# mLSTM cell and mixture of depths on one core: decay exponents built by matmul instead of by broadcast loads

## The chip, the cores and the metric

The kernel runs on one core of a Trainium2 chip. The metric is the time of one execution on the device, in microseconds (us). Before the change it is 265.21 us, the median of three runs (263.96 to 266.42). Engines are named as in the profile: PE (TensorE, with PEld for its weight loads), DVE (VectorE), ACT (ScalarE), POOL (GpSimd), SP (SyncE, which here only issues transfers).

## The reference

Two stages follow one another. The first is an mLSTM cell over B=4 batches, H=8 heads, S=768 time steps and head size D=40, with a running maximum `m` that keeps the exponents in bounds:

```python
for t in range(S):
    m_new = np.maximum(f_gate[:, :, t] + m, i_gate[:, :, t])
    f_stab = np.exp(f_gate[:, :, t] + m - m_new)
    i_stab = np.exp(i_gate[:, :, t] - m_new)
    m = m_new
    C = f_stab * C + i_stab * outer(vt, kt)
    n = f_stab * n + i_stab * kt
    y[t] = sigmoid(o_gate[t]) * (C @ qt) / max(|n . qt|, 1)
```

The heads are laid side by side: x has 4 x 768 rows of 320. The second stage gives each row a score x . w_gate, picks the 128 highest rows of each batch, and replaces each picked row by x + sigmoid(score) * (relu(x @ w1) @ w2), with w1 320x1024 and w2 1024x320. All is float32.

## The kernel before

**Tiling.** The time axis is cut into NT=6 chunks of L=128 steps, so there are 24 steps (b, c) in the outer loop (L371), batch after batch. Within a chunk the recurrence is written as matmuls: a masked weight W (source step by target step, per head) multiplies k.q, and the product P times v gives the chunk's own share; the state C, carried from chunk to chunk, gives the rest. A column of ones beside v (D1 = 41) carries the normaliser n.

**Prologue (L84 to L159).** The gates of all 32 (batch, head) rows lie on 32 partitions. For each of the six chunks DVE scans F (sums of f), a = i - F and Mg (running maximum of a), ACT takes the exponentials r and wk, PE transposes a, wk and r to columns (`cols`), and Mg with r's last value behind it is stored to a scratch `M_d[c]` in DRAM.

**Loads (L95 to L103, L350).** For a step, SP issues k, q and v (160 KB each, in runs of 160 bytes) and then `Mb`, which reads eight rows of `M_d` into all 128 partitions (516 KB). NB=4 buffers, AHEAD=2 steps ahead. The o gates of a batch are six further loads (`so`), issued at the batch's start for the first batch and at c = 3 for the next; ACT turns them into sigmoids (L364).

**A step, `mlstm_chunk` (L174 to L255).** POOL masks Mb (L177). ACT makes W in eight exponentials, one per head (L181). PE transposes k and q (L188), ACT copies them out (L189). PE computes pS (L198), DVE multiplies with W into P (L200). PE reads the state, pI (L207), and DVE scales it by r into `num` (L210). POOL scales v (wv, L215), PE makes the state's addition pC (L221), DVE decays C by the value carried in Mb and adds pC (L229, L231). PE makes pH from P and v (L236) and DVE adds it to `num` (L240). DVE forms the denominator and its reciprocal (L243 to L246), POOL multiplies it with the o gate (`sor`, L248), DVE writes x (L249) and its score (L252). POOL issues two stores of x, one to a scratch `x_d` and one to the output (L255).

**Ranking and the picked rows.** `compare` (L257) adds a chunk's scores to comparisons (`ge`, L265), one step late. `ranks` (L269) and `gather` (L289) pick the rows and fetch them from `x_d` (L301); `layer1` (L307) and `layer2` (L338) are the two products, and L345 scatters the rows to the output. For batches 0 and 1 this is done inside the next batch's steps. After the last step come batch 2's layer1, then batch 3's ranks, batch 2's layer2, batch 3's gather and its two layers (L402 to L406).

**Order.** The engines take their instructions in order. A scheduler in the framework orders the instructions of each engine at build time from the order of the program; buffers of a pool rotate, and an instruction that writes a buffer waits for the last reader of its previous content. PSUM tiles of one tag share two buffers: `t` holds pt, `a` holds pI, pC and pH, `m` the rest, and pS has two of its own.

Of the kernel before, what the change touches and what calls it, by code (L numbers as in the profile page):

```python
# [27 lines left out]
def kernel(  # L28
# [35 lines left out]
    NB = 4  # L64
    GE = [L * u * (u + 1) // 2 for u in range(NT + 1)]
    HALVES = [slice(0, 64), slice(64, 128)]
    AHEAD = 2

    assert S == NT * L and D < DP and H == 2 * NP and BH <= 128 and F_ == NFC * 128 and 0 < capacity < S <= 2048
# [14 lines left out]
    f_sb = gate.tile([BH, NT, L], FP, name="f_sb")  # L84
    i_sb = gate.tile([BH, NT, L], FP, name="i_sb")
    nc.sync.dma_start(out=f_sb, in_=f_gate.rearrange("b h (c p) -> (b h) c p", p=L))
    nc.sync.dma_start(out=i_sb, in_=i_gate.rearrange("b h (c p) -> (b h) c p", p=L))
# [3 lines left out]
    for n in range(NB):  # L91
        nc.gpsimd.memset(qk_t[n][:, :, :, D:DP], 0.0)
        nc.gpsimd.memset(v_t[n][:, :, D:DP], 1.0)

    def load_chunk(b, c):  # L95
        n = (b * NT + c) % NB
        t = slice(c * L, (c + 1) * L)
        for j, src in enumerate((k, q)):
            nc.sync.dma_start(out=qk_t[n][:, j, :, 0:D], in_=src[b, :, t, :].rearrange("h p d -> p h d"))  # L99
        nc.sync.dma_start(out=v_t[n][:, :, 0:D], in_=v[b, :, t, :].rearrange("h p d -> p h d"))  # L100
        Mb = work.tile([128, H, L + 1], FP, name="Mb", bufs=NB)
        nc.sync.dma_start(out=Mb, in_=_bcast(M_d[c][b * H:(b + 1) * H, :], 128))
        return qk_t[n], v_t[n], Mb  # L103

    ident = const.tile([128, 128], FP, name="ident")
    make_identity(nc, ident)
    iota_i = const.tile([128, capacity], I32, name="iota_i")
    nc.gpsimd.iota(iota_i, pattern=[[1, capacity]], channel_multiplier=0)
    iota_f = const.tile([128, capacity], FP, name="iota_f")
    nc.vector.tensor_copy(out=iota_f, in_=iota_i)  # L110

    token_i = const.tile([128, NT], I32, name="token_i")
    nc.gpsimd.iota(token_i, pattern=[[L, NT]], channel_multiplier=1)
    token = const.tile([128, NT], HF, name="token")
    nc.vector.tensor_copy(out=token, in_=token_i)
    later = const.tile([128, NT], FP, name="later")
    nc.vector.tensor_scalar(out=later, in0=token_i, scalar1=-1.0, scalar2=float(S - 1), op0=OP.mult, op1=OP.add)
    earlier = const.tile([128, NT * L], BF, name="earlier")
    nc.gpsimd.memset(earlier, 1.0)
    nc.gpsimd.affine_select(out=earlier[:, S - L:], in_=earlier[:, S - L:], compare_op=OP.is_gt, fill=0.0, base=0,  # L120
                            pattern=[[-1, L]], channel_multiplier=1)
    ones_b = const.tile([128, 1], BF, name="ones_b")
    nc.gpsimd.memset(ones_b, 1.0)
    xe_t = [const.tile([128, NDC * 128], FP, name=f"xe{n}") for n in range(2 * len(SLOTS))]
    n_xe = [0]
    for n in range(len(xe_t)):
        nc.gpsimd.memset(xe_t[n], 0.0)
    x_d = [dram.tile([S, DM], FP, name=f"x_d{b}") for b in range(B)]
    ones = const.tile([BH, L], FP, name="ones")
    nc.vector.memset(ones, 1.0)  # L130


    F = gate.tile([BH, NT, L], FP, name="F")
    a = gate.tile([BH, NT, L], FP, name="a")
    Mg = gate.tile([BH, NT, L + 1], FP, name="Mg")
    r = gate.tile([BH, NT, L], FP, name="r")
    wk = gate.tile([BH, NT, L], FP, name="wk")
    m = gate.tile([BH, NT + 1], FP, name="m")
    nM = gate.tile([BH, NT], FP, name="nM")
    nc.vector.memset(m[:, 0:1], -BIG)  # L140
    M_d, cols = [], []
    for c in range(NT):
        nc.vector.tensor_tensor_scan(out=F[:, c, :], data0=ones, data1=f_sb[:, c, :], initial=0.0,
                                     op0=OP.mult, op1=OP.add)
        nc.vector.tensor_tensor(out=a[:, c, :], in0=i_sb[:, c, :], in1=F[:, c, :], op=OP.subtract)
        nc.vector.tensor_tensor_scan(out=Mg[:, c, 0:L], data0=ones, data1=a[:, c, :], initial=m[:, c:c + 1],
                                     op0=OP.mult, op1=OP.max)
        nc.vector.tensor_tensor(out=m[:, c + 1:c + 2], in0=F[:, c, L - 1:L], in1=Mg[:, c, L - 1:L], op=OP.add)
        nc.vector.tensor_scalar(out=nM[:, c:c + 1], in0=Mg[:, c, L - 1:L], scalar1=-1.0, scalar2=None, op0=OP.mult)
        nc.scalar.activation(out=r[:, c, :], in_=Mg[:, c, 0:L], func=AF.Exp, bias=m[:, c:c + 1], scale=-1.0)  # L150
        nc.scalar.activation(out=wk[:, c, :], in_=a[:, c, :], func=AF.Exp, bias=nM[:, c:c + 1], scale=1.0)
        nc.vector.tensor_copy(out=Mg[:, c, L:L + 1], in_=r[:, c, L - 1:L])
        M_d.append(dram.tile([BH, L + 1], FP, name=f"M_d{c}"))
        nc.scalar.dma_start(out=M_d[c], in_=Mg[:, c, :])
        pc = ps_t.tile([128, 3, BH], FP, name="pc", tag="t")
        for j, row in enumerate((a, wk, r)):
            nc.tensor.transpose(pc[:, j, :], row[:, c, :], ident[0:BH, 0:BH])
        cols.append(const.tile([128, 3, BH], FP, name=f"cols{c}"))
        nc.vector.tensor_copy(out=cols[c], in_=pc)  # L159
# [5 lines left out]
    nc.gpsimd.dma_start(out=wg, in_=_bcast(moe_w_gate, 128))  # L165
# [8 lines left out]
    def mlstm_chunk(b, c, qk, v1, Mb, C, so, x, sc):  # L174
        hs = slice(b * H, (b + 1) * H)
        k_n, q_n = qk[:, 0], qk[:, 1]
        nc.gpsimd.affine_select(out=Mb[:, :, 0:L], in_=Mb[:, :, 0:L], compare_op=OP.is_ge, fill=BIG, base=0,  # L177
                                pattern=[[0, H], [1, L]], channel_multiplier=-1)
        W = work.tile([128, NP, 2, L], FP, name="W")
        for h in range(H):  # L180
            nc.scalar.activation(out=W[:, h // 2, h % 2, :], in_=Mb[:, h, 0:L], func=AF.Exp,  # L181
                                 bias=cols[c][:, 0, b * H + h:b * H + h + 1], scale=-1.0)

        qkT = work.tile([128, 2, NP, L], FP, name="qkT", bufs=2)
        for j in range(2):
            pt = ps_t.tile([128, NP, L], FP, name="pt", tag="t")
            for p in range(NP):
                nc.tensor.transpose(pt[:, p, :], qk[:, j, 2 * p:2 * p + 2, :].rearrange("s a d -> s (a d)"), ident)  # L188
            nc.scalar.copy(out=qkT[:, j], in_=pt)  # L189


# [3 lines left out]
        for p in range(NP):  # L195
            for j in range(2):
                e = HALVES[j]
                nc.tensor.matmul(pS[j][:, p, :], qkT[e, 0, p, :], qkT[e, 1, p, :], start=True, stop=True)  # L198
        for j in range(2):
            nc.vector.tensor_tensor(out=P[:, :, j, :], in0=pS[j], in1=W[:, :, j, :], op=OP.mult)  # L200

        num = None
        if c > 0:
            pI = ps_a.tile([128, H, DP], FP, name="pI", tag="a")
            for p in range(NP):
                for t in HALVES:
                    nc.tensor.matmul(pI[t, 2 * p:2 * p + 2, :].rearrange("t a d -> t (a d)"), qkT[:, 1, p, t],  # L207
                                     C[:, p].rearrange("e a d -> e (a d)"), start=True, stop=True)
            num = work.tile([128, H, D1], FP, name="num")
            nc.vector.tensor_tensor(out=num, in0=pI[:, :, 0:D1], op=OP.mult,  # L210
                                    in1=cols[c][:, 2, hs].unsqueeze(2).to_broadcast([128, H, D1]))

        if c < NT - 1:
            wv = work.tile([128, H, D1], FP, name="wv", bufs=2)
            nc.gpsimd.tensor_tensor(out=wv, in0=v1[:, :, 0:D1], op=OP.mult,  # L215
                                    in1=cols[c][:, 1, hs].unsqueeze(2).to_broadcast([128, H, D1]))
# [5 lines left out]
            decay = Mb.rearrange("p (n a) t -> p n a t", a=2)  # L222
            for j in range(2):
                e = slice(j * DP, j * DP + D)
                Cj, pj = C[e, :, j, 0:D1], pC[e]
                if c == 0:
                    nc.vector.tensor_copy(out=Cj, in_=pj)
                else:
                    nc.vector.tensor_tensor(out=Cj, in0=Cj, op=OP.mult,  # L229
                                            in1=decay[e, :, j, L:L + 1].to_broadcast([D, NP, D1]))  # L230
                    nc.vector.tensor_tensor(out=Cj, in0=Cj, in1=pj, op=OP.add)  # L231

        pH = ps_a.tile([128, H, DP], FP, name="pH", tag="a")
        for h in range(H):
            for t in HALVES:
                nc.tensor.matmul(pH[t, h, :], P[:, h // 2, h % 2, t], v1[:, h, :], start=True, stop=True)  # L236
        if num is None:
            num = pH
        else:
            nc.vector.tensor_tensor(out=num, in0=num, in1=pH[:, :, 0:D1], op=OP.add)  # L240
# [192 lines left out]
```

## Time and profile before

| | |
|---|---|
| median of three runs | 265.21 us |
| profiled execution | 263.01 us |
| its span, first to last instruction | 261.3 us |
| busy: PE, DVE, ACT, POOL | 189.9, 148.7, 120.1, 105.5 us |
| mean granted TensorE clock | 0.88 of full |
| moved by DMA | 41.07 MB, 107085 packets, of which 101328 under 512 bytes |

The profiled execution took 1.7 us more than its span and 2.2 us less than the median. The first x is written at 25.5 us, the second at 48.2, the last (of 24) at 217.7; what follows to 261.3 us is the tail. In lists of groups a row gives line, engine, operation, output and inputs with shapes, count, busy us with mean ns of one, and the engine's idle time before such instructions. In timelines the two leading numbers are start and duration in us.

### The profile page before, as it was taken

The numbers are of one execution on the slowest core, as the hardware profiler recorded it, in microseconds if no ns is written. First come the engines' busy times: TensorE is split into PE (matmuls) and PEld (weight loads), VectorE is DVE, ScalarE is ACT, GpSimd is POOL, SyncE is SP. The second block draws the span as 40 slices with busy tenths as digits, with TensorE's granted clock in tenths as the row PEclk, the third lists the DMA queues.
The fourth block names the chain that finished last, engine by engine and source line by source line (L and its number), as shares of the span: only waits on it lengthen the run. The fifth ranks groups of instructions, "written<-read, shape, count | busy, mean of one in ns | idle before, by whom it ended". The sixth has DMA issues, their size and how long they took to land.

```text
span 261.3 us, 6263 instructions
## 1 busy us (share of the span) xinstructions
PE 189.9 (73%) x2402; PEld 160.6 (61%) x2402; DVE 148.7 (57%) x443; ACT 120.1 (46%) x304; POOL 105.5 (40%) x155
## 2 busy tenths in 40 slices
PE   0498204875987968899799687998969862982980
PEld 0376103764966856887687576976859752961950
DVE  5813303687767998831779799347876985021000
ACT  2484049776568455760556578237633300000000
POOL 8435322635365455643643655443354222003001
PEclk9999855797799988799999979999995995798696
DMA  8979899999799899996599999717533121001000
GB/s 119 147 272 222 288 205 226 224 194 238 163 238 264 198 203 230 238 185 227 102 177 215 221 211 258 222 75 152 130 81 113 41 75 50 3 0 50 3 0 25
DMA packets 107085, 41.07 MB, mean 157 GB/s; under 512 B 101328, under 2 KB 101520, under 8 KB 107056
## 3 DMA queue, kind: packets, MB, share of 16 engines
q1 hardware_dynamic: 103392, 28.61, 55.8%
q0 software_dynamic: 3376, 11.96, 13.6%
q8 instruction: 19, 0.31, 0.5%
q10 hardware_dynamic: 288, 0.10, 0.2%
q14 instruction: 10, 0.08, 0.1%
HBM read 32.05 MB, written 8.62 MB: 156 GB/s over the span
## 4 chain that ended last, share of the span: by engine, by line
issue 23%; DMA 20%; DVE 19%; PE 12%; SPq 10%; POOL 10%; ACT 2%; POOLq 1%; ACTq 0%; DVEq 0%
DMA Mb<-M_d 10%; POOL sor L248 5%; SPq L350 5%; PE pH L236 3%; DVE P L200 3%; DVE x L249 3%; SPq L100 3%; DMA out_dram<-x 3%; PE ph L331 2%; DMA qk<-in_k_dram 2%; SPq L99 2%; DVE ge L265 2%; POOL Mb L177 2%; DMA so<-in_o_gate_dram 2%; DVE C L229 2%
## 5 line engine op out<-in xcount | busy, mean ns | idle before, releaser
L181 ACT ACTIVATE W<-Mb,cols 128x128 f32<-128x128 f32 x192 | 61.2, 392 | 22.8 <-POOL Mb L177 11.8
L236 PE MATMUL pH<-v,P 128*64 128x64 f32 x768 | 30.9, 232 | 24.9 <-DVE P L200 19.7
L236 PEld LDWEIGHTS pH<-v,P 128*64 128x64 f32 x768 | 26.5, 144 | 30.9 <-issue 15.4
L200 DVE TENSOR_TENSOR P<-pS,W 128x512 f32<-128x512 f32 x48 | 31.9, 680 | 17.0 <-ACT W L181 16.6
L177 POOL TENSOR_SCALAR_AFFINE_SELECT Mb<-Mb 128x1024 f32<-128x1024 f32 x24 | 26.9, 1121 | 35.8 <-DMA Mb<-M_d 35.0
L198 PE MATMUL pS<-qkT 64*128 64x128 f32 x384 | 35.6, 319 | 3.0 <-ACT qkT L189 3.0
L188 PE MATMUL pt<-ident,qk 128*128 128x128 f32 x192 | 35.2, 309 | 1.1 <-ACT qkT L189 0.8
L198 PEld LDWEIGHTS pS<-qkT 64*128 64x128 f32 x384 | 29.3, 216 | 7.9 <-ACT qkT L189 4.2
L248 POOL TENSOR_TENSOR sor<-so,rec 128x320 f32<-128x320 f32 x24 | 17.3, 722 | 40.8 <-DVE rec L246 31.7
L189 ACT COPY qkT<-pt 128x512 f32<-128x512 f32 x48 | 26.9, 581 | 14.3 <-PE pt L188 14.2
L331 PE MATMUL ph<-xeT,w 128*128 128x128 f32 x192 | 27.1, 311 | 3.0 <-DVE xeT L323 1.6
L331 PEld LDWEIGHTS ph<-xeT,w 128*128 128x128 f32 x192 | 26.3, 225 | 4.1 <-DVE xeT L323 2.2
L188 PEld LDWEIGHTS pt<-ident,qk 128*128 128x128 f32 x192 | 23.4, 154 | 4.1 <-ACT qkT L189 1.4
L207 PE MATMUL pI<-C,qkT 128*64 128x128 f32 x320 | 25.3, 307 | 0.0
L249 DVE TENSOR_TENSOR x<-num,sor 128x320 f32<-128x320 f32 x20 | 11.4, 570 | 18.9 <-POOL sor L248 18.9
L215 POOL TENSOR_TENSOR wv<-v,cols 128x328 f32<-128x328 f32 x20 | 15.1, 754 | 17.3 <-PE pC L221 6.5
L207 PEld LDWEIGHTS pI<-C,qkT 128*64 128x64 f32 x320 | 20.0, 154 | 2.9 <-issue 0.8
L265 DVE SCALAR_TENSOR_TENSOR ge<-sb,sc,earlier 128x128 bf16<-128x128 f32 (+5 forms) x24 | 19.9, 830 | 2.9 <-ACT sb L263 2.4
L255 POOL DMA_DIRECT2D x_d<-x x24 | 14.1, 590 | 17.7 <-DVE x L249 17.1
L262 PE MATMUL pb<-ident,sc 128*128 128x128 f32 x24 | 8.5, 356 | 15.8 <-DVE sc L252 15.8
L344 DVE SCALAR_TENSOR_TENSOR ye<-py,g,xe 128x320 f32<-128x320 f32 x4 | 2.2, 550 | 30.8 <-PE py L342 30.8
L263 ACT COPY sb<-pb 128x128 f32<-128x128 f32 x24 | 6.2, 260 | 28.5 <-PE pb L262 28.5
(84 smaller groups left out, 250.1 us busy)
## 6 DMA issues: line engine op xcount, KB each, us to landing
Mb<-M_d SPq DMA_DIRECT2D x24, 516.0 KB, 5.6
qk<-in_k_dram SPq DMA_DIRECT2D x24, 160.0 KB, 5.1
qk<-in_q_dram SPq DMA_DIRECT2D x24, 160.0 KB, 5.0
v<-in_v_dram SPq DMA_DIRECT2D x24, 160.0 KB, 4.5
so<-in_o_gate_dram SPq DMA_DIRECT2D x24, 160.0 KB, 4.6
x_d<-x POOLq DMA_DIRECT2D x24, 160.0 KB, 3.2
out_dram<-x POOLq DMA_DIRECT2D x24, 160.0 KB, 3.6
w<-in_moe_w_dram POOLq DMA_DIRECT2D x1, 1280.0 KB, 12.8
```

Source lines behind the costliest of these rows:

```text
L177: nc.gpsimd.affine_select(out=Mb[:, :, 0:L], in_=Mb[:, :, 0:L], compare_op=OP.is_ge, fill=BIG, base=0, pattern=[[0, H], [1, L]], channel_m ...
L181: nc.scalar.activation(out=W[:, h // 2, h % 2, :], in_=Mb[:, h, 0:L], func=AF.Exp, bias=cols[c][:, 0, b * H + h:b * H + h + 1], scale=-1.0)
L188: nc.tensor.transpose(pt[:, p, :], qk[:, j, 2 * p:2 * p + 2, :].rearrange("s a d -> s (a d)"), ident)
L189: nc.scalar.copy(out=qkT[:, j], in_=pt)
L198: nc.tensor.matmul(pS[j][:, p, :], qkT[e, 0, p, :], qkT[e, 1, p, :], start=True, stop=True)
L200: nc.vector.tensor_tensor(out=P[:, :, j, :], in0=pS[j], in1=W[:, :, j, :], op=OP.mult)
L207: nc.tensor.matmul(pI[t, 2 * p:2 * p + 2, :].rearrange("t a d -> t (a d)"), qkT[:, 1, p, t], C[:, p].rearrange("e a d -> e (a d)"), start= ...
L236: nc.tensor.matmul(pH[t, h, :], P[:, h // 2, h % 2, t], v1[:, h, :], start=True, stop=True)
L248: nc.gpsimd.tensor_tensor(out=sor, in0=so[:, c], in1=rec.unsqueeze(2).to_broadcast([128, H, D]), op=OP.mult)
L249: nc.vector.tensor_tensor(out=x[:, c, :].rearrange("p (h d) -> p h d", d=D), in0=num[:, :, 0:D], in1=sor, op=OP.mult)
L265: nc.vector.scalar_tensor_tensor(out=ge[:, GE[u]:GE[u + 1]], in0=sb.rearrange("p t l -> p (t l)")[:, 0:n], scalar=sc[:, u:u + 1], in1=earl ...
L331: nc.tensor.matmul(ph[:, f, :], w1[:, j, (f0 + f) * 128:(f0 + f + 1) * 128], xeT[:, j, :], start=(j == 0), stop=(j == NDC - 1))
```

## The change

- The gates are loaded four times, on four groups of 32 partitions (G), in a first part for chunk 0 and a second for chunks 1 to 5; f by SP and i by ACT's queue. `gates(0, 1)` runs, then chunk 0 is prepared, then `gates(1, NT)` does five chunks in one go, with scans that restart at chunk borders.
- `split` writes a and Mg as bf16: groups 0 and 1 hold the rounded value, group 2 the rest after one rounding, group 3 the rest after two. Group 1 is not used by `pos` and `neg`, which sum groups 0, 2 and 3.
- `prepare` makes the exponents a - Mg of a chunk in PSUM (`pW`): per four heads one matmul with a3 as weights and 512 columns of `pos`, and four with `neg` as weights and M3 as the 128 columns. ACT takes two exponentials of 128x512 from PSUM, POOL masks W after that. `M_d`, `Mb` and their loads are gone.
- q is scaled by r on POOL (`qr`) and transposed as a third block, so that the state's read and the chunk's own product add up in one PSUM tile pH. `num` and its two DVE instructions are gone; x and the denominator read pH.
- The decay of C is one POOL instruction into the next of three buffers, by `left`, a table of r's last values that goes to DRAM and back once; DVE only adds pC.
- `prepare(n+1)` stands behind `mlstm_chunk(n)` in the program. NB is 5, AHEAD 3. Constants and memsets of the prologue move behind chunk 0's preparation.
- x is stored once, to the output; gather reads its rows there. In the tail batch 3's ranks and gather come ahead of batch 2's two layers.

```diff
-    NB = 4
+    NB = 5
-    AHEAD = 2
+    AHEAD = 3
...
+    def load_f_i(c0, c1):
+        for dst, src, eng in ((f_sb, f_gate, nc.sync), (i_sb, i_gate, nc.scalar)):
+            for g in G:
+                eng.dma_start(out=dst[g, c0:c1], in_=src.rearrange("b h (c p) -> (b h) c p", p=L)[:, c0:c1])
...
-        Mb = work.tile([128, H, L + 1], FP, name="Mb", bufs=NB)
-        nc.sync.dma_start(out=Mb, in_=_bcast(M_d[c][b * H:(b + 1) * H, :], 128))
...
+    def split(eng, x3, x, g):
+        eng.tensor_copy(out=x3[:, g], in_=x[:, g])
+        eng.tensor_tensor(out=rest[64:128, g], in0=x[64:128, g], in1=x3[64:128, g], op=OP.subtract)
+        eng.tensor_copy(out=x3[64:128, g], in_=rest[64:128, g])
+        eng.tensor_tensor(out=x3[96:128, g], in0=rest[96:128, g], in1=x3[96:128, g], op=OP.subtract)
+
+    def gates(c0, c1):
...
+        split(nc.vector, M3, Mg, g)
+        split(nc.gpsimd if c0 else nc.vector, a3, a, g)
...
+    def prepare(b, c, qk, v1):
+        hs = slice(b * H, (b + 1) * H)
+        W = work.tile([128, H, L], FP, name="W")
+        for h0 in range(0, H, 4):
+            pW = ps_t.tile([128, 4, L], FP, name="pW", tag="t")
+            nc.tensor.matmul(pW, a3[:, c, :], pos[:, b * H + h0:b * H + h0 + 4].unsqueeze(2).to_broadcast([128, 4, L]),
+                             start=True, stop=False)
+            for h in range(4):
+                n = b * H + h0 + h
+                nc.tensor.matmul(pW[:, h, :], neg[:, n:n + 1].to_broadcast([128, L]), M3[:, c, :], start=False,
+                                 stop=(h == 3))
+            nc.scalar.activation(out=W[:, h0:h0 + 4, :], in_=pW, func=AF.Exp)
+        nc.gpsimd.affine_select(out=W, in_=W, compare_op=OP.is_ge, fill=0.0, base=0, pattern=[[0, H], [1, L]],
+                                channel_multiplier=-1)
+        srcs = [qk[:, 0], qk[:, 1]]
+        if c > 0:
+            qr = qr_t[c % 2]
+            nc.gpsimd.tensor_tensor(out=qr[:, :, 0:D], in0=qk[:, 1, :, 0:D], op=OP.mult,
+                                    in1=cols[c][:, 1, hs].unsqueeze(2).to_broadcast([128, H, D]))
+            srcs.append(qr)
...
+        for j, src in enumerate(srcs):
+            pt = ps_t.tile([128, NP, L], FP, name="pt", tag="t")
+            for p in range(NP):
+                nc.tensor.transpose(pt[:, p, :], src[:, 2 * p:2 * p + 2, :].rearrange("s a d -> s (a d)"), ident)
+            nc.scalar.copy(out=T[:, j], in_=pt)
+        return W, T, wv
...
-        num = None
-        if c > 0:
-            pI = ps_a.tile([128, H, DP], FP, name="pI", tag="a")
...
-            num = work.tile([128, H, D1], FP, name="num")
-            nc.vector.tensor_tensor(out=num, in0=pI[:, :, 0:D1], op=OP.mult,
-                                    in1=cols[c][:, 2, hs].unsqueeze(2).to_broadcast([128, H, D1]))
+                    nc.tensor.matmul(pH[t, 2 * p:2 * p + 2, :].rearrange("t a d -> t (a d)"), T[:, 2, p, t],
+                                     C[:, p].rearrange("e a d -> e (a d)"), start=(p == 0), stop=False)
...
-                    nc.vector.tensor_tensor(out=Cj, in0=Cj, op=OP.mult,
-                                            in1=decay[e, :, j, L:L + 1].to_broadcast([D, NP, D1]))
+                nc.gpsimd.tensor_tensor(out=Cn[:, :, :, 0:D1], in0=C[:, :, :, 0:D1], op=OP.mult,
+                                        in1=left[:, hs, c].rearrange("p (n a) -> p n a", a=2).unsqueeze(3)
+                                        .to_broadcast([128, NP, 2, D1]))
...
-            nc.vector.tensor_tensor(out=num, in0=num, in1=pH[:, :, 0:D1], op=OP.add)
...
-        for dst in (x_d[b], out[b]):
-            nc.gpsimd.dma_start(out=dst[c * L:(c + 1) * L, :], in_=x[:, c, :])
+        nc.gpsimd.dma_start(out=out[b, c * L:(c + 1) * L, :], in_=x[:, c, :])
...
+    load(0)
+    load_f_i(1, NT)
+    gates(0, 1)
+    prepared(0)
+    gates(1, NT)
+    left_d = dram.tile([BH, NT], FP, name="left_d")
+    nc.scalar.dma_start(out=left_d, in_=r[:, :, L - 1])
+    left = const.tile([128, BH, NT], FP, name="left")
+    nc.sync.dma_start(out=left, in_=_bcast(left_d, 128))
...
+        mlstm_chunk(b, c, *ready[n], *state[b][0])
+        if n + 1 < N:
+            prepared(n + 1)
...
-    before_last = layer1(B - 2, todo) if B > 1 else []
-    sels = ranks(B - 1, *state[B - 1][1][2:])
-    layer2(B - 2, before_last)
-    layer2(B - 1, layer1(B - 1, gather(B - 1, sels)))
+    picked = gather(B - 1, ranks(B - 1, *state[B - 1][1][2:]))
+    if B > 1:
+        layer2(B - 2, layer1(B - 2, todo))
+    layer2(B - 1, layer1(B - 1, picked))
```

## The prediction, made before the changed kernel was run

> **What bounds the kernel now.** First the page's slices. In the first 26 of 40 (to 170 us) the DMA row stands at 7 to 9 nearly throughout, while PE and DVE move between 4 and 9; in the last seven only PE works. PEclk is below 9 wherever PE has paused.
>
> ```profile
> PE   0498204875987968899799687998969862982980
> ...
> DVE  5813303687767998831779799347876985021000
> ...
> PEclk9999855797799988799999979999995995798696
> DMA  8979899999799899996599999717533121001000
> ```
>
> Then the queues, for what a transfer costs, and the list of waits, for who suffers.
>
> ```profile
> q1 hardware_dynamic: 103392, 28.61, 55.8%
> q0 software_dynamic: 3376, 11.96, 13.6%
> ```
> ```profile
> POOL Mb L177 <- DMA Mb<-M_d: 35.0, 18, 4.9
> ```
>
> q0 moved 11.96 MB in 13.6% of 261.3 = 35.5 us of all 16 engines, 0.337 MB per us. If Mb (24 x 0.528 MB, long pieces) goes at that rate, it takes 1.57 us each, 37.7 in all; of q1's 145.8 us some 108 remain for 96 loads of k, q, v and o in 160-byte pieces, 1.12 each. A step then needs 4 x 1.12 + 1.57 + two stores at 0.49 = **7.0 us of DMA**. The x of DVE gives the step really taken:
>
> ```profile
> 48.20 0.49 DVE L249 TENSOR_TENSOR x<-num,sor 128x320 f32<-128x320 f32 x1 [2.19 <-POOL sor L248]
> ```
> ```profile
> 217.71 0.49 DVE L249 TENSOR_TENSOR x<-num,sor 128x320 f32<-128x320 f32 x1 [0.90 <-POOL sor L248]
> ```
>
> 22 steps in 169.5 us. Two gaps (113.58 to 129.74 and 165.56 to 178.66) hold the layers of the picked rows and are 15.3 us longer than two plain steps; the other time is 154.2 / 22 = 7.0 us. So DMA bounds the body. Where loads are finished (from 199 us) a step takes 6.84 and 6.08; DVE bounds there: 148.7 / 24 = 6.2.
>
> PE's timeline gives its warm prices, taken from start to start since matmuls overlap: pH 1.08, pS 1.09, pI 0.93, pC 0.54; eight transposes end to end at 111.15 give 0.125 each; pb 0.16. A step is 4.8 us.
>
> ```profile
> 202.74 1.15 PE L236 MATMUL pH<-v,P 128*64 128x64 f32 x32
> 203.82 1.16 PE L198 MATMUL pS<-qkT 64*128 64x128 f32 x16
> 204.91 1.09 PE L207 MATMUL pI<-C,qkT 128*64 128x128 f32 x16
> 205.84 0.61 PE L221 MATMUL pC<-wv,qk 128*64 128x41 f32 x16
> 206.38 0.87 PE L188 MATMUL pt<-ident,qk 128*128 128x128 f32 x6
> ```
>
> **What the Trainium skill says.** "TensorE: Matmul & The Clock Gate", Part 1 on the clock gate: PE runs at half clock after a few idle microseconds. The trace agrees: pS took 2.08 us at 45.83, after a pause of 14.85, and 1.16 at 203.82. The same page, "Wait — 56ns, not 53.3ns?" and "Back-to-back issue gap", prices bf16: 216 ns for 512 columns, 56 to 81 for 128. No matmul of that kind is in this trace; the nearest, 21 pairs of bf16 weight load and one column (pcol), start in 0.53 us, 25 ns each, so the weight load is not the bound. "DMA: Bandwidth & Descriptors", Specifications: pieces under 512 B lose rate; 0.164 MB in 1.12 us here is 0.146 MB per us against 0.337. "ScalarE: Activation LUTs", What ACT_TABLE_LOAD costs: 1283 ns and a drain of 1380; here the load takes 1.28 and the activation follows at once (36.26 and 37.55), so I take 1.28.
>
> **The change part by part.** *DMA.* Out go Mb (1.57 a step) and one store (0.49); the quadrupled gates add 0.6 MB once. A step needs 4.95 us: DMA is no longer the bound. Gathering from the output instead of x_d is one indirect read as before: nothing, as both wait for the same stores.
>
> *DVE.* Per step it loses both num (0.49 + 0.49) and the decay (0.37 x 2): 6.2 becomes about 4.5. Nothing on the path.
>
> *ACT.* Eight exponentials at 0.31 start to start (2.45) become two of 128x512 from PSUM; nearest row L189, 0.58 each. The third copy adds 0.58. 3.2 us in all.
>
> *POOL.* Out: a DMA issue (0.59) and the memset of C; in: qr (like sor, 0.72) and the decay (like wv, 0.75). 4.6 us.
>
> *PE.* In: pW, 2 x (0.22 + 4 x 0.07 + first weights 0.03) = 1.05 (bounds 0.9 and 1.2), and four transposes of qr, 0.5. PE's step is 4.8 + 1.55 = **6.35 us**, and it will be warm.
>
> *The cycle.* In the order built for the changed kernel PE does pW, pW, pt of k and q, pb, pt of qr, pS, state read, pC, pH and then the next step's pW. Preparation is not placed beside the DVE wait of the step before. Five PSUM tiles of a step go through the two buffers of tag t, each held until ACT has emptied it. With t = 0 at pW: exp 0.67 to 1.25 and to 1.83; pt of q may start at 1.88, its copy ends at 3.10; pS 3.15 to 4.24; P 4.39 to 5.75 (0.68 each); state read and pC fill PE until 5.71; pH 5.80 to 6.88. POOL's mask fits (1.9 to 3.0), so does DVE's chain den to ge (0.15 to 4.3, against P at 4.39). So the step is **6.9 us** (bounds 6.35, PE alone, and 7.5, with 0.1 more at each of six hand-overs): the DMA's 7.0 is replaced by nearly the same.
>
> *What this uncovers.* The layers in the body cost PE 5.5 + 4.4 + 0.4 = 10.2 us each, as nothing else is late: 20.4 against 15.3 before. The sigmoids: 1.28 + 1.80 + 1.28 = 4.36 us of ACT. Before they lay beside DMA waits; in the new order two stand between the halves of W, on the cycle; the first has about 2 us. 10.7 in all (bounds 2 and 13). Ranks, 0.7 of PE per batch, fit into the cycle's 0.5 of waiting: 0. If that cover is gone, 2 us.
>
> *Start.* Before, W of step 1 waited on ACT for the sigmoid:
>
> ```profile
> 36.26 1.28 ACT L364 ACT_TABLE_LOAD   x1 [13.42 <-DMA so<-in_o_gate_dram]
> 37.55 1.27 ACT L364 ACTIVATE so<-so 128x1280 f32<-128x1280 f32 x1
> ```
>
> Now chunk 0's gates end at about 8 us (18 short DVE operations at 0.13 to 0.47 from 4 us). The five-chunk part has eight operations of 640 columns at about 0.8 (from L200, 0.68 for 512) and two scans at up to five times 0.40 and 0.47: 10.7 us, with P and pC's copies between, to 22. `left_d` takes 3.8 like M_d; SP waits for it with the last `so` load queued behind `left`, and ACT's sigmoid waits for that load (4.6): 31. Then 1.27 + 1.28, and W of step 1 starts at 33.6 against 40.1: x of step 1 at about 41.5 (bounds 37 and 45) against 48.2, **-6.7**. POOL's late memsets and weight loads lie beside DVE's work.
>
> *Tail.* Before, ye of batch 3 came 36 us after the last x. The gather stood open:
>
> ```profile
> 239.69 0.87 PE L321 MATMUL pX<-ident,xe 128*128 128x128 f32 x3 [5.17 <-DMA xe<-x_d,idx]
> 241.22 8.05 PE L331 MATMUL ph<-xeT,w 128*128 128x128 f32 x48 [0.65 <-DVE xeT L323]
> ```
>
> From py's end (234.3) to ph, 6.9 us, 1.4 will remain. But ranks, sel and pidx now stand ahead of the first ph, which moves from 221.3 to 224.5. POOL issues the gather before any scatter, so no queue stands before it. **-2.9**.
>
> *Sum.* Body 22 x 6.9 + 20.4 + 10.7 = 182.9 against 169.5, +13.4; start -6.7; tail -2.9: **+3.8 us** on the profiled 263.01. On the median, 2.2 above that execution, 269.0.
>
> **The rivals.** *A, the forecast:* PE's ordered cycle replaces DMA; its own range 262 to 278. Chance 0.52. *B, faster:* the cycle closes up to 6.5 because PE's reordered weight loads and ACT's copies overlap more than I assume, and the sigmoids cost 5. For it: PE's work is 6.35 and its clock was only 0.88. Against it: five tiles in two buffers. Body 143 + 20.4 + 5 = 168.4, -1.1; start -8; tail -2.9: 253. It decides from a step of 6.6 down, each 0.1 being 2.2 us. Chance 0.31. *C, clearly slower:* POOL becomes the bound. It does the mask, sor, qr, wv, the decay and the store's issue in order, and waits inside that row for x and for DVE's C. For it: sor already waited 31.7 us for rec. Against it: 4.6 of 6.9. A step of 7.5 gives 22 x 0.6 more, 282. Chance 0.17. That DMA stays the bound is possible too, since 160-byte loads remain, but at 4.95 it would have to be priced 40% too low; its time would be A's.
>
> **How the numbers follow.** The likeliest is 269. The range goes down to B (252 with the early start) and up to C, 283. About 1% can be told from no change. Faster by over 1% (below 262.6): most of B and a little of A, 0.30; within: 0.15; slower: most of A and all of C, 0.55.
>
> **What would show it.** Right: no waits for Mb; DMA row at 6 to 7 in the body; PE busy over 215 us with clock near 1; x every 6.9 us; pt or pS of PE waiting for ACT; sigmoids opening gaps of 4 us; first x of step 1 near 41. Wrong: PE with idle between pH and pW, POOL busy without gaps, steps under 6.6, or a DMA row still at 9.

## The result, and the profile after

The changed kernel takes 289.0 us (287.7 to 290.2, four runs) beside 264.9 for the kernel before (264.0 to 266.4): ratio 1.090, 95% interval 1.083 to 1.098. It is slower; 269.0 was forecast, in a range of 252 to 283. Times are medians of all executions, but some executions of any of these kernels fall into a slower state, so ratios compare the undisturbed ones alone; b_tail, b_both and b_decay below have only one of these and hence no ratio, and their profiles, like a_ahead's, are of disturbed ones.

The page's slices of the changed kernel, as tenths of each fortieth of the span:

```profile
PE   0445306878988849789999296899999988729891
...
DVE  2599101666656715562287243560396856651100
...
PEclk9985555999999959999999869799999999977999
DMA  5999999944459913435079426153141010000000
```

DMA's row is full in slices 2 to 8 and again in 13, 14 and 22, and stands at 0 to 5 in most of the rest; PE's is mostly at 7 to 9 from slice 8 on, with holes at 15, 23 and 36. PE is low up to slice 6, and its clock is at 0.5 in slices 4 to 7. The queues show what went:

```profile
q1 hardware_dynamic: 100368, 16.23, 40.2%
q0 software_dynamic: 2224, 8.03, 8.7%
```

12.4 MB less on q1, 3.9 MB less on q0. The list of waits (total, times, longest) has no Mb any more. In its place stand:

```profile
ACT W L204 <- PE pW L202: 45.6, 16, 5.0
...
PEld pt L222 <- ACT W L204: 25.7, 15, 11.6
...
ACT L394 <- DMA so<-in_o_gate_dram: 18.4, 3, 16.1
```

The first is slack of ACT. The second is PE standing before the transposes until the exponentials have emptied pW. The third has one wait of 16.1 us, which lies in the start. The span grew from 261.3 to 286.0 us. Cut at the x of step 1 (54.14) and of step 23 (251.04):

| part | predicted change | measured change |
|---|---|---|
| start, to x of step 1 | -6.7 | +5.9 (54.1 against 48.2) |
| body, 22 steps | +13.4 | +27.4 (196.9 against 169.5) |
| tail, after x of step 23 | -2.9 | -8.6 (35.0 against 43.6) |
| sum | +3.8 | +24.7 |

**The start** in the timeline of the changed kernel (start, duration, engine, line, and the idle time before it with what ended it):

```profile
25.10 0.65 ACTq L425 DMA_DIRECT2D left_d<-F  x1
...
35.93 0.35 SPq L427 DMA_DIRECT2D left<-left_d  x1
36.32 0.43 SPq L382 DMA_DIRECT2D so<-in_o_gate_dram  x1
...
41.15 1.28 ACT L394 ACT_TABLE_LOAD   x1 [16.08 <-DMA so<-in_o_gate_dram]
42.44 1.27 ACT L394 ACTIVATE so<-so 128x1280 f32<-128x1280 f32 x1
43.73 1.28 ACT L204 ACT_TABLE_LOAD   x1
...
45.02 1.08 ACT L204 ACTIVATE W<-pW 128x512 f32<-128x512 f32 x2
45.67 1.56 PEld L222 LDWEIGHTS pt<-ident,qk 128*128 128x128 f32 x8 [11.62 <-ACT W L204]
```

One load of o gates stands on SP behind `left`, which waited 10.8 us for the small write `left_d`; ACT holds the sigmoid of steps 2 to 5 until its gates have landed; W of step 1 stands behind that sigmoid, and PE behind W. PE had the first half of pW done by 33.5.

**A plain step** (the preparation of step 4, same view):

```profile
69.80 1.14 PE L222 MATMUL pt<-ident,qk 128*128 128x128 f32 x8 [0.30 <-ACT W L204]
70.00 0.49 DVE L283 TENSOR_TENSOR x<-pH,sor 128x320 f32<-128x320 f32 x1 [0.84 <-POOL sor L282]
70.30 1.09 POOL L205 TENSOR_SCALAR_AFFINE_SELECT W<-W 128x1024 f32<-128x1024 f32 x1 [0.34 <-ACT W L204]
70.53 1.21 DVE L286 CUSTOM_DVE_ANT_0 scr<-x,wg 128x320 f32<-128x320 f32 x1
...
71.80 0.32 PE L295 MATMUL pb<-ident,sc 128*128 128x128 f32 x1 [0.86 <-DVE sc L286]
...
72.49 1.16 PE L236 MATMUL pS<-T 64*128 64x128 f32 x16
...
77.41 1.14 PE L222 MATMUL pt<-ident,qk 128*128 128x128 f32 x8 [0.30 <-ACT W L204]
```

From pt to pt it is 7.61 us. PE waits 0.86 for the score of the step just ended, because pb stands between the transposes of q and k and those of qr. And the score is late because `scr` takes 1.21 us, not the 0.49 that it took before (mean 505 ns): it lies across POOL's mask and ends 0.35 us after it. The Trainium skill, "SBUF — State Buffer", Who interferes with whom, states this case: a VectorE operation with two inputs in SBUF and a GpSimd operation that reads SBUF contend for ports that the two engines share, and the one that comes second is blocked until the other ends. The trace agrees nearly: fully blocked, `scr` would end 0.49 us after the mask, and it ends 0.35 after. It holds in the other direction too: POOL's qr takes 1.13 us at 72.66, begun behind DVE's `ge`, and 0.72 at 105.94, alone.

**A sigmoid** of the next batch's gates falls between the two halves of W:

```profile
98.83 1.28 ACT L394 ACT_TABLE_LOAD   x1 [0.89 <-DMA so<-in_o_gate_dram]
100.12 1.80 ACT L394 ACTIVATE so<-so 128x1920 f32<-128x1920 f32 x1
101.94 1.28 ACT L204 ACT_TABLE_LOAD   x1
...
103.89 1.12 PE L222 MATMUL pt<-ident,qk 128*128 128x128 f32 x4 [4.21 <-ACT W L204]
...
105.79 2.02 PE L236 MATMUL pS<-T 64*128 64x128 f32 x16
```

PE waits 4.21 us, and its clock is low afterwards: pS takes 2.02 us instead of 1.16.

### The profile page after: what moved, and what is told of

Its sections match the earlier page's. It is cut to its first block, busy times and chain, and to the rows that moved or that the text cites. A ratio compares the mean times of both kernels' runs of the same rounds, so it can differ in the third digit from the quotient of the medians.

```text
span 286.0 us, 6679 instructions
## 1 busy us (share of the span) xinstructions
PE 211.5 (74%) x2716; PEld 174.5 (61%) x2716; DVE 137.3 (48%) x363; ACT 98.4 (34%) x172; POOL 126.5 (44%) x174
## 5 line engine op out<-in xcount | busy, mean ns | idle before, releaser
L204 ACT ACTIVATE W<-pW 128x512 f32<-128x512 f32 x48 | 26.5, 595 | 84.7 <-PE pW L202 45.6
L223 ACT COPY T<-pt 128x512 f32<-128x512 f32 x68 | 38.1, 587 | 16.5 <-PE pt L222 16.3
L205 POOL TENSOR_SCALAR_AFFINE_SELECT W<-W 128x1024 f32<-128x1024 f32 x24 | 28.3, 1177 | 18.8 <-ACT W L204 18.4
L236 PE MATMUL pS<-T 64*128 64x128 f32 x384 | 30.2, 301 | 0.7 <-ACT T L223 0.7
L236 PEld LDWEIGHTS pS<-T 64*128 64x128 f32 x384 | 25.4, 202 | 5.7 <-ACT T L223 2.6
L248 PE MATMUL pH<-C,T 128*64 128x128 f32 x320 | 22.5, 284 | 0.0
L198 PE MATMUL pW<-pos,a 128*128 128x512 bf16 x48 | 19.6, 409 | 3.1 <-DVE pos L119 1.6
L283 DVE TENSOR_TENSOR x<-pH,sor 128x320 f32<-128x320 f32 x24 | 11.8, 491 | 17.9 <-POOL sor L282 17.9
L210 POOL TENSOR_TENSOR qr<-qk,cols 128x320 f32<-128x320 f32 x20 | 16.6, 832 | 8.3 <-PE pt L222 7.1
L202 PE MATMUL pW<-M,neg 128*128 128x128 bf16 x192 | 20.2, 229 | 0.0
```

Of the source, the lines that this page charges most:

```text
L198: nc.tensor.matmul(pW, a3[:, c, :], pos[:, b * H + h0:b * H + h0 + 4].unsqueeze(2).to_broadcast([128, 4, L]), start=True, stop=False)
L202: nc.tensor.matmul(pW[:, h, :], neg[:, n:n + 1].to_broadcast([128, L]), M3[:, c, :], start=False, stop=(h == 3))
L204: nc.scalar.activation(out=W[:, h0:h0 + 4, :], in_=pW, func=AF.Exp)
L205: nc.gpsimd.affine_select(out=W, in_=W, compare_op=OP.is_ge, fill=0.0, base=0, pattern=[[0, H], [1, L]], channel_multiplier=-1)
L223: nc.scalar.copy(out=T[:, j], in_=pt)
L236: nc.tensor.matmul(pS[j][:, p, :], T[e, 0, p, :], T[e, 1, p, :], start=True, stop=True)
```

## The experiments

Names that begin with a are edits of the changed kernel (289.0, ratio 1.090), with b of the kernel before. Ratios are to runs of the kernel before on the same chip, where it took 264.9 to 267.1 us. All parts come from one profile each:

| run | time, us | ratio [interval] | x of step 1 | body | tail |
|---|---|---|---|---|---|
| changed | 289.0 | 1.090 [1.083, 1.098] | 54.1 | 196.9 | 35.0 |
| a_left | 288.0 | 1.086 [1.080, 1.093] | 52.6 | 198.1 | 36.2 |
| a_pb | 284.7 | 1.078 [1.071, 1.084] | 54.1 | 192.6 | 35.3 |
| a_mask | 284.3 | 1.072 [1.065, 1.080] | 54.5 | 193.8 | 35.2 |
| a_tanh | 282.8 | 1.068 [1.061, 1.074] | 56.7 | 190.2 | 34.7 |
| a_all | 279.0 | 1.044 [1.039, 1.050] | 50.4 | 191.2 | 35.7 |
| a_weights | 290.5 | 1.088 [1.083, 1.093] | 45.2 | 207.7 | 35.9 |
| a_best | 277.9 | 1.050 [1.041, 1.060] | 44.2 | 194.7 | 35.6 |
| a_ahead | 283.8 | 1.070 [1.062, 1.078] | 50.6 | 199.3 | 36.0 |
| a_sig | 277.9 | 1.050 [1.040, 1.061] | 48.1 | 193.8 | 34.6 |
| a_final | 277.8 | 1.050 [1.041, 1.060] | 44.1 | 196.6 | 35.7 |
| before | 264.9 | 1 | 48.2 | 169.5 | 43.6 |
| b_tail | 261.7 (256.5 to 266.0) | none | 47.9 | 175.0 | 37.7 |
| b_xonce | 267.3 | 0.998 [0.989, 1.006] | 47.1 | 175.7 | 42.9 |
| b_noq | 268.7 (263.8 to 275.5) | 1.003 [0.998, 1.007] | 46.5 | 175.3 | 43.7 |
| b_both | 261.3 (256.2 to 262.0) | none | 47.0 | 175.9 | 36.0 |
| b_best | 260.9 | 0.984 [0.976, 0.992] | 39.5 | 185.4 | 35.7 |
| b_decay | 268.4 (263.5 to 269.5) | none | 47.5 | 175.9 | 44.1 |
| b_spread | 252.5 | 0.953 [0.945, 0.962] | 40.4 | 176.5 | 36.0 |
| b_win | 251.1 | 0.949 [0.940, 0.957] | 40.1 | 173.7 | 35.9 |

The profiles of the b runs, b_best apart, have bodies of about 175 us where the one profile of before had 169.5, whatever the edit; differences of body below 6 us between them are not read. The body's +27.4 above carries the same doubt.

### Four single remedies, and all together

**a_left**, the load of `left` behind the o gates on SP:

```diff
-    nc.sync.dma_start(out=left, in_=_bcast(left_d, 128))
...
             sigmoid(state[0][0][0], EARLY, NT)
+            nc.sync.dma_start(out=left, in_=_bcast(left_d, 128))
```

> The changed kernel, with the load of the table of decays (left) issued after the o-gate loads instead of ahead of the last of them. Theory 1, the wait in SP's queue delays the start: the scratch write that left waits for took 10.8 us (25.1 to 35.9), the last o-gate load stood behind it and ACT's sigmoid behind that load. Without it the sigmoid can start near 30 and W of step 1 is then held by the split of a on POOL, which ended at 32.4: first x of step 1 at 42 to 45 instead of 54.1, time 8 to 12 us less. Theory 2, the loads themselves are late because the weights share the DMA engines: the sigmoid still starts after 37, at most 4 us less.

The last o gates of the group are issued by 25.3 instead of 36.32, and the table load of their sigmoid still starts at 39.41: they take that long to land. The intervals of the two kernels overlap, and x of step 1 comes 1.5 us earlier, not 9 to 12: the order on SP was not what held the start.

**a_pb**, `compare` ahead of the next preparation, pb in tag t:

```diff
+        if n > 0:
+            compare(*steps[n - 1], *state[steps[n - 1][0]][1])
         if n + 1 < N:
             prepared(n + 1)
-        if n > 0:
-            compare(*steps[n - 1], *state[steps[n - 1][0]][1])
...
-        pb = ps_m.tile([128, L], FP, name="pb", tag="m")
+        pb = ps_t.tile([128, L], FP, name="pb", tag="t")
```

> The changed kernel, with the transpose of a chunk's scores (pb) emitted one step later and rotating in the PSUM tag of the other transposes, so that PE meets it right after the next step's pH, when the scores are long there. Theory 1, PE waits in its order for the scores: 0.86 us and a little more in every plain step go; the plain step is 6.7 instead of 7.6, time 10 to 16 us less. Theory 2, POOL or DVE is the bound and PE's wait only shows it: another wait takes its place, the step stays above 7.4, under 4 us.

In the timeline pb starts with no wait, right behind pH, and the step is 7.1 us:

```profile
68.98 1.14 PE L222 MATMUL pt<-ident,qk 128*128 128x128 f32 x8 [0.22 <-ACT W L204]
...
74.59 0.32 PE L295 MATMUL pb<-ident,sc 128*128 128x128 f32 x1
...
76.09 1.14 PE L222 MATMUL pt<-ident,qk 128*128 128x128 f32 x8 [0.22 <-ACT W L204]
```

So the wait is real, 0.5 us a plain step. Only 4.3 us come of it in all, between the two theories: the two gaps with a sigmoid are 15.3 and 16.4 us instead of 13.6 and 14.7, and the steps before them take 6.1 instead of 4.8.

**a_mask**, the mask as a fifth bf16 matmul in PSUM that adds -1e30 above the diagonal, POOL's operation gone:

```diff
+            nc.tensor.matmul(pW, ident_b, causal.unsqueeze(1).to_broadcast([128, 4, L]), start=False, stop=True)
...
-        nc.gpsimd.affine_select(out=W, in_=W, compare_op=OP.is_ge, fill=0.0, base=0, pattern=[[0, H], [1, L]],
-                                channel_multiplier=-1)
```

> The changed kernel, with POOL's mask of W taken away: a fifth kind of matmul adds -1e30 to the masked exponents in PSUM (0.22 us of PE more per half of W, 0.44 per step). Theory 1, POOL's mask lengthens DVE's score operation (1.21 us beside the mask, 0.49 without) and PE waits for that score: the score goes back to 0.5, PE's wait for it falls from 0.9 to about 0.2, less 0.44 for the matmuls: 3 to 8 us less. Theory 2, POOL is the bound, as the third rival of the prediction had it: 1.1 us per step go, some 20 us less. Theory 3, neither: 8 to 10 us more, the price of the matmuls.

The groups by form, changed kernel and then a_mask (busy us, mean ns):

```profile
L286 DVE CUSTOM_DVE_ANT_0 scr<-x,wg 128x320 f32<-128x320 f32 x24 | 19.4, 807 | 0.7
```
```profile
L291 DVE CUSTOM_DVE_ANT_0 scr<-x,wg 128x320 f32<-128x320 f32 x24 | 11.9, 494 | 0.7
```

With POOL's operation gone `scr` is back at 494 ns, and in a plain step pb no longer waits:

```profile
70.96 0.29 PE L300 MATMUL pb<-ident,sc 128*128 128x128 f32 x1
```

The step is 7.1 us although PE does two matmuls more. The gain of 4.7 us is that of theory 1 (3 to 8). POOL is not the bound (theory 2, rival C's cause, asked for 20 us): the edit removes the same wait as a_pb from its other end.

**a_tanh**, the sigmoid as 0.5 + 0.5 tanh(x/2), with one DVE operation per batch:

```diff
-        nc.scalar.activation(out=so[:, c0:c1], in_=so[:, c0:c1], func=AF.Sigmoid)
+        nc.scalar.activation(out=so[:, c0:c1], in_=so[:, c0:c1], func=AF.Tanh, scale=0.5)
+        nc.vector.tensor_scalar(out=so[:, c0:c1], in0=so[:, c0:c1], scalar1=0.5, scalar2=0.5, op0=OP.mult, op1=OP.add)
```

> The changed kernel, with the sigmoid of the o gates computed as 0.5 + 0.5 tanh(x/2), which needs no change of ACT's table, and one DVE operation per batch for the halves. Theory 1, the sigmoids with their two table loads stand in PE's cycle: each of three becomes 1.8 us instead of 4.36 and PE's clock does not fall after it; two gaps of 13.6 and 14.7 us between x become 9 to 10; 8 to 13 us less. Theory 2, ACT has room and the gaps come from the o-gate loads: under 3 us less.

The Trainium skill, "ScalarE: Activation LUTs", Table sets, lists tanh in the same set as exp. The trace agrees: one ACT_TABLE_LOAD is left of eleven, and ACT is busy 85.6 us instead of 98.4. The body is 6.7 us shorter, but the two gaps are still 12.8 and 12.3 us, where theory 1 had 9 to 10: the table loads are a part of what a sigmoid costs here, not all of it.

> The changed kernel with all four edits at once: pb met right after pH, the mask as a fifth bf16 matmul in PSUM, sigmoid as a tanh, the load of left behind the o-gate loads. Alone they gave -4.3, -4.7, -6.2 and -1.0 us. Theory 1 (each takes a separate wait out of one in-order PE stream): they add, 289.0 - 16.2 = 273, range 270 to 276. Theory 2 (one shared limit, each edit only moves the wait): no more than the best pair, 278 to 283.

a_all's 279.0 us lies in theory 2's range, but the kernel before took longer on that chip too (267.1). In ratio a_all is 0.046 below the changed kernel, where the four alone sum to 0.057: they add to four fifths. That a_pb and a_mask share one wait would account for a shortfall; it was not tested as a pair.

### The start

**a_weights**, a_left with the expert weights held until a score exists:

```diff
+            nc.gpsimd.tensor_copy(out=w1[0:w, j, 0:1], in_=late[0:w])
             nc.gpsimd.dma_start(out=w1[0:w, j, :], in_=moe_w1[d0:d0 + w, :])
...
-        if n == 1:
-            load_weights()
+        if n == 3:
+            load_weights(state[0][1][0][:, 1:2])
```

> a_left (288.0), and the expert weights are not loaded until the score of step 1 exists (a copy of one element into each weight tile makes the load wait), some 40 us later than now. Theory 1 (the first 40 us are DMA-bound: the o-gate loads issued at 20.7 landed at 39.4 because 3.4 MB of weights pass beside them): x of step 1 from 52.6 to 44-47, total 280 to 283. Theory 2 (the start is held by something else, or the weights only take the bandwidth later from the body): x of step 1 at 50 or later, total 286 to 291.

x of step 1 comes at 45.2, and the loads of o gates take at most 8.2 us to land in the start where one took 14.7: they had been late because of what passed beside them. But the built order changed as well. W of step 1 stands ahead of that sigmoid on ACT now (33.71 against 36.97 us), so this run does not separate the two. And 19.5 us lie between steps 2 and 3. The timeline:

```profile
63.52 1.28 ACT L396 ACT_TABLE_LOAD   x1 [8.49 <-DMA so<-in_o_gate_dram]
64.82 1.80 ACT L396 ACTIVATE so<-so 128x1920 f32<-128x1920 f32 x1
66.53 0.57 ACT L225 COPY T<-pt 128x512 f32<-128x512 f32 x1
...
67.24 1.97 PE L250 MATMUL pH<-C,T 128*64 128x128 f32 x16 [10.23 <-ACT T L225]
```

The o gates of the second batch, not needed for three steps, now met the weights, and their sigmoid stood on ACT ahead of the copy that PE wanted. Neither theory was whole: the start came as early as theory 1 had it, and the total is no better than theory 2's.

**a_best** (a_all, weights after the score of step 3) and **a_ahead** (AHEAD 2):

> a_all (279.0) with the expert weights not loaded until the score of step 3 exists, so that they pass neither beside the first o-gate loads nor beside those of the second batch. Theory 1 (what is left in the start is DMA bandwidth, and the stop of a_weights at its step 3 was a sigmoid that sat on ACT ahead of PE's copies while its loads competed with the weights): x of step 1 at 43 to 46 instead of 50.4, no gap above 10 us among the first eight steps, total 269 to 274. Theory 2 (the lost time comes back wherever the weights pass): 277 to 284.

> The changed kernel with AHEAD 2 as before instead of 3 (five buffers stay). Theory 1 (the start is late because one more step of k, q and v, 3 x 1.12 us of DMA, lands ahead of the o gates that the first big sigmoid waits for): x of step 1 from 54.1 to 50-51, total 284.5 to 287.5. Theory 2 (the order of these loads doesn't matter, only what passes in all, or left): x of step 1 at 53 or later, total 288 to 291.

a_best has x of step 1 at 44.2, and gaps of 12.6 and 10.6 us further on; at 277.9 us (theory 2) it is no faster than a_all. a_ahead has x of step 1 at 50.6, the figure of its theory 1, but by another path. With these gates issued ahead of the weights, their sigmoid starts at 26.74 instead of 41.15 and W of step 1 at 34.33 instead of 45.02. Then DVE waits for the mask on POOL, which stands behind a decay of C that waits for `left`:

```profile
46.00 1.29 DVE L238 TENSOR_TENSOR P<-pS,W 128x512 f32<-128x512 f32 x2 [12.64 <-POOL W L205]
```

After x of step 1 comes a gap of 15.8 us with a_weights' picture: ACT's table load `[4.15 <-DMA so<-in_o_gate_dram]` at 57.16, PE's state read `[6.18 <-ACT T L223]`. Its ratio is nevertheless 0.02 below the changed kernel's; its one profile doesn't tell where from.

**a_sig** changes only this order: each later sigmoid takes as its bias a zero made from the last copy of a step.

```diff
+            bias = work.tile([128, 1], FP, name="zero")
+            nc.scalar.activation(out=bias, in_=T[:, j, 0, 0:1], func=AF.Copy, scale=0.0)
...
         if n + 1 < N:
             prepared(n + 1)
+        if n == 0:
+            sigmoid(state[0][0][0], EARLY, NT, ready[1][3], 2)
+        if c == NT - 1 and b + 1 < B:
+            sigmoid(state[b + 1][0][0], 0, NT, ready[n + 1][3], 1)
```

> The changed kernel with each later sigmoid held behind the last copy of transposes of a step (its bias is a zero that ACT makes from that copy): steps 2 to 5 of the first batch behind step 1, each later batch behind its own first step. Theory 1 (ACT runs in order: the sigmoid that waits for its o gates stands ahead of the W of step 1, which PE has had ready since 33, and in a_weights, a_best and a_ahead ahead of PE's copies): the wait of 11.4 us before pt of step 1 falls below 4, x of step 1 from 54.1 to 44-47, total 279 to 283. Theory 2 (bandwidth alone: the loads that step 1 or 2 needs are late whatever stands first on ACT): x of step 2 stays at 60 or later, total 286 to 291.

It is the largest gain of a single edit, 0.040 in ratio or some 11 us; in the profiles 6.0 us of it lie in the start and 3.1 in the body. W of step 1 starts at 33.30 instead of 45.02, with the weights where they were. x of step 1 falls to 48.1, not to 44 to 47; a second wait shows behind the first:

```profile
33.30 0.60 ACT L204 ACTIVATE W<-pW 128x512 f32<-128x512 f32 x1 [2.27 <-PE pW L202]
...
39.62 0.75 POOL L259 TENSOR_TENSOR C<-C,left 128x328 f32<-128x328 f32 x1 [6.09 <-DMA left<-left_d]
...
42.39 1.09 POOL L205 TENSOR_SCALAR_AFFINE_SELECT W<-W 128x1024 f32<-128x1024 f32 x1
...
43.51 1.29 DVE L238 TENSOR_TENSOR P<-pS,W 128x512 f32<-128x512 f32 x2 [11.18 <-POOL W L205]
```

POOL holds the decay of C until `left` lands, and the mask of step 1 stands behind it, as in a_ahead. So `left` does cost, on POOL and not on SP, once ACT's order is mended.

> All remedies in the changed kernel: a_all, the sigmoids held behind the copies as in a_sig, and the weights in five parts as in b_spread. Theory 1 (what a_best lost, two gaps of 12.6 and 10.6 us, were sigmoids ahead of copies): 277.9 - 10 = 263 to 270. Theory 2 (the lost time comes back in the body): 273 to 279. On either theory it does not reach b_win's 251, as 22 steps of 6.7 to 7.5 us remain.

a_final starts as early as a_best (44.1) and ends where a_sig does, in theory 2's range. A loss comes back before x of step 3, again in order behind a load, this time of v on POOL:

```profile
62.15 0.74 POOL L226 TENSOR_TENSOR wv<-v,cols 128x328 f32<-128x328 f32 x1 [6.66 <-DMA v<-in_v_dram]
```

With every remedy in it the changed kernel is still 5.0% slower than the one before. Its start is earlier and its tail shorter; the body, 196.6 us against 170 to 176, holds the rest, and no run shows what would shorten it.

### What bounds the kernel before

**b_xonce** and **b_noq** take DMA away. In b_noq 20 of 24 loads of q are left out, so it computes something else:

```diff
-        for j, src in enumerate((k, q)):
+        for j, src in enumerate((k, q) if b * NT + c < NB else (k,)):
```

> The kernel before with nothing but x stored once and gathered from the output. Theory 1 (DMA bounds the body of before; each store is 0.49 us of the 16 engines' time): -0.49 x 22 = -8 to -11 where it bounds all the way, at least -5: 254 to 260. Theory 2 (the body of before is held by its chain of engines, DMA hidden in it): -2 to +1, 263 to 266.

> The kernel before, with q loaded only for the first four steps; later steps use the q that lies in their buffer. This leaves 20 of the 24 loads of q out, 1.12 us of the 16 engines each by the prediction's sum, so its time is that of another output. Theory 1 (the throughput of DMA bounds the body of before, as predicted: 7.0 us a step): steps fall to DVE's 6.2, -0.8 x 20 = -16, 248 to 254. Theory 2 (b_xonce showed that it does not; a busy DMA row is waiting, not a bound): -4 to +1, 261 to 268.

Nothing is gained, with the interval of b_noq at 0.998 to 1.007, though its queue carries less:

```profile
q1 hardware_dynamic: 82592, 25.34, 46.0%
```

It is 46.0% of the engines' time instead of 55.8%, and the time stayed: DMA's throughput does not bound the body of before. **b_decay**, DVE's multiply of C on POOL:

> The kernel before with the decay of C, two DVE multiplies of 0.37 us or more a step, issued to POOL instead. Theory 1 (b_xonce and b_noq ruled DMA out; DVE, 148.7 us of work and in the chain P, num, den, x, is what bounds the body of before): -0.5 to -0.7 x 20 = -10 to -14, 251 to 256. Theory 2 (no one engine bounds it; each step is a chain over PE, DVE, POOL and ACT in which this piece has slack, and POOL's share slows DVE): -3 to +4, 262 to 269.

DVE is busy 141.1 us instead of 148.7, and the fastest run, 263.5 us, is no faster than the fastest of before (262.8): DVE's load alone isn't the bound either, though POOL got the work. What sets 6.6 to 7 us a step there was not shown by an experiment. A chain over PE, DVE, POOL and ACT is one candidate. The time that a single load takes to land is another: DMA and SP's issues make 30% of the chain that ended last in the page of before and 20% in b_noq's.

### The tail, and a kernel that beats both

**b_tail** is before with the changed kernel's last lines; **b_both** adds the single store; **b_best** delays the weights as in a_best.

> The kernel before with nothing but the changed kernel's tail: ranks and gather of the last batch first, then the layers of the last but one. Theory 1 (the order of the tail alone made the change's 8.6 us: PE stays at work between the two layer blocks): -6 to -9, 256 to 259. Theory 2 (the tail was shorter for other reasons, such as x stored once or a free DMA ring): -3 to +1, 262 to 266.

> The kernel before with the changed tail and with x stored once, nothing else. Theory 1 (the tail's order gives 5 to 6 us, the single store nothing): 259 to 262 beside a before of 265. Theory 2 (the store is worth something once the tail is short): 254 to 258.

> b_both, and the expert weights not loaded until the score of step 3 exists. Theory 1 (the start of before is DMA-bound too: x of step 1 at 48.2 behind a sigmoid that waits for the o gates): x of step 1 at 42 to 44, total 252 to 257 beside a before of 265. Theory 2 (the weights then take the same time from the body): 259 to 264.

The fastest runs of b_tail and b_both take 256.5 and 256.2 us, where the fastest of before on their chips took 266.0 and 263.5. Their profiles have tails of 37.7 and 36.0 us against 43.6, and b_best's and b_spread's have 35.7 and 36.0: the order makes most of the change's 8.6. The single store makes about 2 of it. From the issue of the last scatter to the end it is 6.8 to 6.9 us in before and b_tail and 4.9 to 5.1 in b_xonce, b_both, b_best, b_spread and the changed kernel; why was not looked into.

b_best starts 8.7 us earlier, is 13 ahead at step 5 (x at 65.5 against 78.8), and loses it in a gap of 17.5 while 3.4 MB of weights pass at once; its 260.9 us are theory 2's. **b_spread** loads them in five parts, each behind one score:

```diff
+        if n in (3, 4, 5, 6, 7):
+            load_weights(n - 3, state[0][1][0][:, n - 2:n - 1])
```

> b_both with the expert weights in five parts, each loaded once the score of one of the steps 1 to 5 exists, instead of all at 12 to 20 us (before) or all at 60 us (b_best). Theory 1 (b_best lost its earlier start, x of step 5 at 65.5 instead of 78.8, because 3.4 MB came at once and held Mb): x of step 1 at 40 to 44, x of step 6 at 78 or earlier, total 252 to 257. Theory 2 (the body has no room for them, however they are spread): 259 to 264.

> b_spread and b_decay together. Theory 1 of both: 243 to 250. Theory 2 of b_decay with theory 1 of b_spread: 252 to 258. Neither: 260 to 266.

b_spread is 4.7% faster than before, b_win 5.1%; their intervals overlap, so b_decay's part isn't told from nothing. In the profiles the start is 8 us earlier and the tail 8 shorter than before's, and the body is that of the other b runs.

## Why the prediction was wrong

**Start: the term of -6.7 was +5.9.** The chain was named as it ran: gates, `left_d`, SP, the last load of o gates, sigmoid, W. Along it the sizes failed. `left_d` was put at 3.8 us "like M_d" and took 10.8 (+7.0); it was issued at 25.1 where the sum had 22 (+3.1); the table load, put ahead of the data, came behind it (+1.3); from W to x it was 9.1, with a cold PE, instead of 7.9 (+1.2). These are the 12.6 us. But this is a sum along one chain and not what each link is worth. a_left took SP's link away, and x of step 1 came 1.5 us earlier, since the other gates were late as well. "POOL's late memsets and weight loads lie beside DVE's work" was a cost put at nothing: the weights pass on the DMA engines together with the o gates (8.2 us at most to land without them, 14.7 with them). `left_d` is no such case in the main, as it still took 8.6 us in a_weights. The step that failed most was to take W of step 1 behind that sigmoid as given: a_sig, with the same loads, has W at 33.3, which is what the prediction forecast, and x of step 1 at 48.1. What then keeps it from the forecast 41.5 is the decay of C, which waits for `left` on POOL ahead of the mask, and which the prediction did not have on the path.

**Body: +13.4 was +27.4.** Six steps of the last batch, with neither sigmoid nor layers, take 43.85 us (207.19 to 251.04), 7.31 each instead of 6.9: 22 x 0.41 = +9.0. The cycle had DVE's chain to `ge` fit without loss: `scr` was priced without the mask beside it, and pb was placed where its score is not there yet. It put pS 3.15 us after the step's pW; in step 4 pS comes 4.04 after it (68.45 to 72.49). a_pb and a_mask each take that wait out and give 7.1. Sigmoids were put at 10.7, 4.36 for each of two on the cycle. Steps 7 to 9 and 13 to 15 take 27.3 and 30.5 us where the same steps of the last batch, 19 to 21, take 20.5: together 16.8 more (+6.1). PE's wait and its low clock afterwards belong to it; no run splits them. The two layer blocks cost 16.4 - 7.7 = 8.7 each, not 10.2 (-2.9). That leaves 1.8 unassigned, and the 169.5 of before is itself uncertain by some 6.

**Tail: -2.9 was -8.6.** The working's own figures, 5.5 off the gather's wait and 3.2 for the later ph, come to -2.3. Both came near (5.7 and 2.9). It missed that PE then goes through both layers almost without a pause, so that the second ph takes 5.62 us where it took 8.05:

```profile
270.31 5.62 PE L363 MATMUL ph<-xeT,w 128*128 128x128 f32 x48 [0.78 <-DVE xeT L355]
```

The last scatter, 2.0 us shorter, was not in the sum either.

**The bound of before** was misread: a DMA row at 9 and a sum of 7.0 that met the step were taken as cause. b_xonce and b_noq refute it. The 6.2 us for DVE was misread too: 148.7 / 24 counts prologue and tail with the steps. Neither entered the sum, which used the measured 169.5, but the first made a change that removes DMA look like a trade of equals.

**What was right:** pb, W and sigmoids as places where PE waits; more likely slower than not. No waits for Mb is right by construction. DMA fell lower than 6 to 7, and PE was busy 211.5 us (over 215 was said) at a clock of 0.903. Rival B's closed cycle needed 6.6; a_all reaches it in single steps only. Rival C's 282 was nearest to 289.0, with the wrong cause, as a_mask shows.

## What to carry to other kernels

On an engine that works in order, ask for each operation that waits for a load what stands behind it: activations that only later steps need were worth some 11 us here. Before a busy row is called the bound, take some of its work away and time that. And a load that is delayed needs a place where it fits: on the kernel before, five small parts gained what one late block had lost (b_spread against b_best); in a_final the parts gained nothing.

## What the hardware showed that was not expected

- A write of 192 four-byte pieces took 10.8 us from its issue to the next issue of the queue that waits for it. It was not the weights alone: with these held back it took 8.6 to 9.1 (a_weights, a_best, a_final). M_d's writes of before were taken as 3.8.
- A DVE operation with two SBUF inputs went from 0.49 to 1.21 us when POOL's mask had started 0.23 us before it, and to 0.83 where 0.61 had passed (a_pb, mask from 69.64, `scr` from 70.25); it ended 0.35 us after the mask both times.
- The four bf16 matmuls of 128 columns in a group of pW, each with its own weight load, take 0.23 us from start to start of what follows (68.67 to 68.90), 57 ns each; the prediction allowed 70 and 30 for the first load. pW costs 0.89 us a step, not 1.05.
